# Performer attention, mixture of experts and squared-ReLU layer in one kernel: ten narrowing steps move to the end of a unit and to GpSimd's queue, and one token load is issued earlier

## The chip, the core and the metric

The kernel runs on one core of a Trainium2 chip. The core has five instruction streams that run side by side and meet at semaphores: TensorE (PE in the profile; PEld are its weight loads), VectorE (DVE), ScalarE (ACT), GpSimd (POOL) and SyncE (SP). Each stream executes its own instructions strictly in the order in which they were issued. Transfers are started by SP or by POOL and run on 16 shared DMA engines. The metric is device microseconds of one execution, from a median over runs; lower is better.

## The reference

Three parts follow one another, in float32: linear attention with an exponential feature map, a top-1 mixture of experts, and a feed-forward layer with a squared ReLU.

```python
def _attn_ref(q, k, v, omega):
    ...
    q_p, k_p = (phi(q_s), phi(k_s))
    kv = np.einsum('bhsm,bhsd->bhmd', k_p, v)
    ...
    return (num / den).astype(np.float32)

def _moe_ref(x, w_gate, w1, w2):
    ...
        h = np.maximum(xe @ w1[e], 0.0)
        ye = h @ w2[e]
        out[mask] = gate_w[mask, None] * ye

def _moe2_ref(x, w_in, w_out):
    h = np.maximum(x @ w_in, 0.0)
    return (h * h @ w_out).astype(np.float32)
```

There are 4 batches of 576 tokens, so 2304 tokens of width 512; the last layer has 2048 hidden units. The change concerns only the last layer, `h = relu(x @ w_in)` and `h * h @ w_out`, and there mostly its first product.

## The kernel before

**Stages.** Attention, then the experts (one expert per batch of tokens), then the last layer in two passes. Pass one computes the hidden values of the last layer and stores them to DRAM (`hscr`); pass two reads them back and multiplies by `w_out`. Every matmul operand is split into a rounded high part and a low rest (ACT copies the high part, DVE subtracts: `split`, L688), and each product is three matmuls: high x high, high x low, low x high.

**Pass one** is `first(u)` for units u = 0 to 15. A unit covers a pair of weight tiles for two batches and uses a seven-product scheme for 2x2 blocks. It has 14 *places*: place 2n+i is product n (0 to 6) for batch i (0, 1), six matmuls each, 84 in a unit. The products accumulate in PSUM banks X, Z and Y. Product 0 goes to X, and ACT copies X out as `p1` (`keep`, L920) before product 2 may accumulate onto the same bank. At product 5 DVE adds `Y + p1` (L959), which is the last read of that copy; the copy of the next unit goes to the same bytes of the tile `xT`. At product 3 DVE adds `Z + u2` (L954) into the buffer `h[i]`, which must first have been stored by the unit before (`hscr<-xT`, L966, from SP). The ReLUs with squares are L923 on DVE and L962, L963 on ACT.

**Work beside the matmuls.** After every place `self.extras(SA + 14 * u + 2 * n + i)` runs what the table in `plan` has put there. It is of four kinds:

- *Narrowing.* `w_in` and `w_out` arrive as float64 bits. `narrow_load` (L693) loads one half tile (512 KB, tile `wd`), `narrow` (L703) converts it (one ACT `Abs`, L715, then four DVE operations, L716 to L719) and stores 256 KB to `wscr`. 22 of the 32 are done in the expert stage. The other ten (`self.late`, odd numbers 13 to 31, halves of `w_out` that only pass two reads) are done in units 3 to 12, one per unit, at place 9. They share one buffer (`s0`) and one result buffer (`s1`). Their transfers are issued from SP: in SP's stream the store of one, the load of the next, then the two `hscr` stores of the unit.
- *Tokens.* Batch b, half c (here written token block (b, c)): `x_load` (L884) loads it, `x_sums` (L895) makes four sums on POOL (L69 to L72), `x_split` (L899) makes the high and low parts in four pieces. For b = 3 the load is issued from POOL. Blocks use two raw buffers in turn, so (3, 1) takes the place of (2, 1), and the first half of that place is free when pieces 0 and 1 of (2, 1) have been split.
- *Weight pairs.* `pair_load` (L632, two transfers from POOL), `pair_sums` (four sums on POOL, L60 to L63) and `pair_split`, for pairs p = 2 to 7 in units 2, 3, 6, 7, 10, 11 and the units after them.
- *Loads for pass two*, from place 13 of unit 12 on (`blocks_load`, from POOL).

Units 0 and 1 use batches 0 and 1, unit 2 is the first to use batches 2 and 3. What a place says is only where an instruction stands in each engine's stream: an engine that is idle runs ahead of the matmuls as far as its semaphores let it.

Of the kernel before, what the change touches and what calls it, by code (L numbers as in the profile page):

```python
# [9 lines left out]
I32 = mybir.dt.int32  # L10
# [8 lines left out]
DM = H * D  # L19
# [17 lines left out]
SA = 1000  # L37
# [52 lines left out]
class Kern:  # L90
# [602 lines left out]
    def narrow_load(self, c):  # L693

        f, i = divmod(c, 2)
        if c in self.late:
            st = self.more.tile([P, 2 * DM], F32, tag="s0", name=f"wd{c}", bufs=1).bitcast(I32)
        else:
            st = self.stage(f"wd{c}").bitcast(I32)
        self.nc.sync.dma_start(out=st, in_=self.a["wf"][f, :, i * DM : (i + 1) * DM].bitcast(I32))  # L700
        self.raw["d", c] = st

    def narrow(self, c):  # L703

        nc = self.nc
        f, i = divmod(c, 2)
        st = self.raw.pop(("d", c)).rearrange("p (n w) -> p n w", w=2)
        low, high = st[:, :, 0], st[:, :, 1]
        if c in self.late:
            r = self.more.tile([P, 2 * DM], I32, tag="s1", name=f"narrow{c}", bufs=1)[:, :DM]  # L710
        else:
            r = self.work.tile([P, DM], I32, tag="osb", name=f"narrow{c}", bufs=2)
        rf = r.bitcast(F32)
        v = nc.vector
        nc.scalar.activation(rf, high.bitcast(F32), AF.Abs)  # L715
        v.tensor_scalar(rf, rf, F64_LEAST, F64_MOST, op0=ALU.max, op1=ALU.min)  # L716
        v.tensor_scalar(r, r, 5, 2, op0=ALU.logical_shift_left, op1=ALU.logical_shift_right)
        v.scalar_tensor_tensor(r, high, -(1 << 30), r, op0=ALU.bitwise_and, op1=ALU.bitwise_or)
        v.scalar_tensor_tensor(r, low, 29, r, op0=ALU.logical_shift_right, op1=ALU.bitwise_or)  # L719
        nc.sync.dma_start(out=self.wscr[f][:, i * DM : (i + 1) * DM], in_=rf)  # L720


    def steps(self):
# [94 lines left out]
    def plan(self):  # L818
        ev = self.events = {}

        def at(s, *e):
            ev.setdefault(int(s), []).append(e)

        for f in range(5, NFE):
            at(f - 5, self.expert_split, 0, f)
        n_at = [4 + 45 * i // 21 for i in range(22)] + [SA + 14 * (3 + i) + 9 for i in range(10)]
        w_at = [5, 6, 7] + [s for s in range(8, 80) if s % 8 in (0, 2, 5, 6)]
        order = [2 * f for f in range(NFF)] + [2 * f + 1 for f in range(NFF)]
        self.late = order[22:]
        for n, c in enumerate(order):  # L830
            at(n_at[n] - (13 if c in self.late else 2), self.narrow_load, c)
            at(n_at[n], self.narrow, c)
        for i in range(24):
            b, f = 1 + i // NFE, i % NFE
            at(w_at[i] - 2, self.expert_load, b, f)
            at(w_at[i], self.expert_split, b, f)

        for i in range(4):
            b, c, u = i // 2, i % 2, 48 + 2 * i
            at(u, self.x_load, b, c)  # L840
            at(u + 2, self.x_sums, b, c)
            for j in range(4):
                at(u + 3 + j // 2, self.x_split, b, c, j)
        at(57, self.pair_load, 1, 0)
        at(58, self.pair_sums, 1, 0)
        for i in range(4):
            at(60 + i // 2, self.pair_split, 1, 0, i)

        at(61, self.pair_load, 1, 1)
        at(62, self.pair_sums, 1, 1)  # L850
        for i in range(4):
            at(SA + 2 + i, self.pair_split, 1, 1, i)
        beside = ((1, 4, 9, 10, 11, 12), (5, 9, 14, 15, 16, 17), (12, 16, 20, 21, 22, 23), (17, 21, 25, 25, 26, 27))
        for i, (l, m, *f) in enumerate(beside):
            b, c = 2 + i // 2, i % 2
            at(SA + l, self.x_load, b, c)
            at(SA + m, self.x_sums, b, c)
            for j in range(4):
                at(SA + f[j], self.x_split, b, c, j)
        for p in range(2, NP):  # L860
            u = SA + 14 * (4 * (p // 2 - 1) + 3 + p % 2)
            at(u - 6, self.pair_load, 1, p)
            at(u - 2, self.pair_sums, 1, p)
            for i in range(4):
                at(u + 1 + 2 * i, self.pair_split, 1, p, i)
        for p, l in enumerate((181, 183, 185, 187, 197, 201, 213, 217)):
            at(SA + l, self.blocks_load, p)
        for p in range(7):
            at(SA + (196, 199, 202, 207, 212, 216, 221)[p], self.blocks_split, p)
        for k, l, f in ((0, 204, 210), (1, 209, 219)):  # L870
            at(SA + l, self.h_load, k)
            at(SA + f, self.h_split, k)
        for s in ev:
            ev[s].sort(key=lambda e: ("load" in e[0].__name__) * (1 if e[0] in (self.narrow_load, self.expert_load) else 3) or 2)
# [415 lines left out]
```

## Time and profile before

| | |
|---|---|
| median of 3 runs | 771.57 us |
| the runs | 771.57, 771.61, 767.67 us |
| the profiled execution | 767.86 us, of which the span of instructions is 766.3 us |
| busy in the span | PE 740.9 us (97%), DVE 566.7 (74%), ACT 418.8 (55%), POOL 212.4 (28%) |
| pass one | 375.99 to 570.3 us in the span |
| issue to landing, medians | `we` (512 KB, POOL) 4.8 us, `wd` (512 KB, SP) 4.7, `hscr` store (576 KB, SP) 4.6, `wscr` store (256 KB, SP) 2.3 |

The profile has one profiled execution, so durations below come from that one, and its own time, 767.86 us, is near the lowest of the three runs. TensorE is the engine that is nearly always busy; the other engines' idle time matters only where TensorE waits for them. "Granted clock" is the share of TensorE's full clock, 2.4 GHz, in a stretch; it has a lower level of 1.2 GHz.

### The profile page before, as it was taken

The numbers are of one execution on the slowest core, as the hardware profiler recorded it, in microseconds if no ns is written. First come the engines' busy times: TensorE is split into PE (matmuls) and PEld (weight loads), VectorE is DVE, ScalarE is ACT, GpSimd is POOL, SyncE is SP. The second block draws the span as 40 slices with busy tenths as digits, with TensorE's granted clock in tenths as the row PEclk, the third lists the DMA queues.
The fourth block names the chain that finished last, engine by engine and source line by source line (L and its number), as shares of the span: only waits on it lengthen the run. The fifth ranks groups of instructions, "written<-read, shape, count | busy, mean of one in ns | idle before, by whom it ended". The sixth has DMA issues, their size and how long they took to land. (4 is left out here: it accounts for less than half of the span.)

```text
span 766.3 us, 15766 instructions
## 1 busy us (share of the span) xinstructions
PE 740.9 (97%) x5832; PEld 731.0 (95%) x5832; DVE 566.7 (74%) x1204; ACT 418.8 (55%) x1012; POOL 212.4 (28%) x272
## 2 busy tenths in 40 slices
PE   8999999999999999999988999899999999999995
PEld 7999999999999999999988999899999999999995
DVE  7788877876776667767395857676785899898783
ACT  5777776963554345535465545455573455454451
POOL 4666566831100010046265512201241110000000
PEclk9999998999999999999999999999999999999999
DMA  8756554645866766553244654645677464444330
GB/s 298 242 164 201 183 191 126 183 121 157 277 201 192 248 219 223 174 175 111 69 154 152 214 197 151 221 149 205 216 243 258 164 221 138 138 139 136 120 104 31
DMA packets 77108, 136.14 MB, mean 178 GB/s; under 512 B 8513, under 2 KB 37329, under 8 KB 77025
## 3 DMA queue, kind: packets, MB, share of 16 engines
q1 hardware_dynamic: 67584, 102.35, 40.5%
q0 software_dynamic: 9440, 32.73, 13.7%
q8 instruction: 48, 0.79, 0.4%
q14 instruction: 36, 0.29, 0.1%
HBM read 93.54 MB, written 41.50 MB: 176 GB/s over the span
## 5 line engine op out<-in xcount | busy, mean ns | idle before, releaser
L763 ACT ACTIVATE hh<-h 128x288 fp32r<-128x288 f32 x64 | 26.4, 412 | 98.0 <-PE h L753 97.9
L920 ACT COPY xT<-X 128x288 f32<-128x288 f32 x96 | 37.9, 403 | 54.8 <-PE X L946 32.8
L764 DVE SCALAR_TENSOR_TENSOR hl<-h,hh 128x288 fp32r<-128x288 f32 x64 | 29.1, 455 | 41.8 <-ACT hh L763 41.3
L1014 ACT CAST hc<-xT 128x384 fp32r<-128x384 f32 (+1 forms) x76 | 38.8, 563 | 28.5 <-DVE xT L63 20.4
L272 ACT ACTIVATE kp<-pj_kp,bias_kp 128x128 f32<-128x128 f32 x144 | 39.3, 397 | 25.1 <-DVE bias_kp L260 16.8
L618 POOL DMA_DIRECT2D we<-we x32 | 17.7, 552 | 121.1 <-DVE wB L612 54.3
L954 DVE TENSOR_TENSOR xT<-Z,xT 128x288 f32<-128x288 f32 x32 | 14.5, 456 | 44.5 <-DMA hscr<-xT 35.1
L657 POOL DMA_DIRECT2D xT<-wscr x32 | 17.2, 540 | 101.7 <-DVE w L691 43.0
L944 PE MATMUL X<-wA,w 128*128 128x288 f32 x128 | 39.0, 305 | 5.9 <-ACT xT L920 5.3
L1060 PE MATMUL y<-wB,hc 128*128 128x256 f32 x152 | 43.2, 284 | 0.0
L1058 PE MATMUL y<-wB,hc 128*128 128x256 f32 x152 | 43.1, 284 | 0.0
L1059 PE MATMUL y<-wB,hc 128*128 128x256 f32 x152 | 43.0, 283 | 0.0
L1016 DVE TENSOR_TENSOR hc<-xT,hc 128x384 fp32r<-128x384 f32 (+1 forms) x76 | 42.2, 617 | 0.0
L944 PE MATMUL X<-wB,w 128*128 128x288 f32 x128 | 38.2, 298 | 3.5 <-ACT wB L690 2.7
L272 ACT ACTIVATE qp<-pj_qp,bias_qp 128x128 f32<-128x128 f32 x144 | 39.3, 394 | 3.2 <-DVE bias_qp L260 1.6
L285 PE MATMUL kv_ps<-vin,kp 128*128 128x65 f32 (+1 forms) x320 | 40.6, 281 | 0.0
L285 PEld LDWEIGHTS kv_ps<-vin,kp 128*128 128x128 f32 (+1 forms) x320 | 38.9, 197 | 1.1 <-issue 0.3
L923 DVE SCALAR_TENSOR_TENSOR xT<-xT 128x288 f32<-128x288 f32 (+1 forms) x64 | 39.2, 644 | 0.0
L752 PE MATMUL h<-xl,wB 128*128 128x288 f32 x128 | 38.1, 298 | 0.9 <-DVE xl L740 0.9
L752 PE MATMUL h<-xl,wA 128*128 128x288 f32 x128 | 37.9, 296 | 0.4 <-DVE xl L740 0.4
L945 PE MATMUL X<-wB,w 128*128 128x288 f32 x128 | 37.9, 296 | 0.4 <-DVE wB L691 0.4
L780 PE MATMUL y<-hl,wA 128*128 128x288 f32 x128 | 37.9, 296 | 0.3 <-DVE hl L764 0.3
(240 smaller groups left out, 3070.7 us busy)
## 6 DMA issues: line engine op xcount, KB each, us to landing
hscr<-xT SPq DMA_DIRECT2D x32, 576.0 KB, 4.6
we<-we POOLq DMA_DIRECT2D x32, 512.0 KB, 4.8
wd<-wf SPq DMA_DIRECT2D x32, 512.0 KB, 4.7
xT<-hscr SPq DMA_DIRECT2D x64, 256.0 KB, 4.4
xT<-wscr POOLq DMA_DIRECT2D x48, 256.0 KB, 4.3
wscr<-narrow SPq DMA_DIRECT2D x32, 256.0 KB, 2.3
vin<-vv SPq DMA_DIRECT2D x18, 260.0 KB, 3.9
kpc<-kk SPq DMA_DIRECT2D x18, 256.0 KB, 3.0
```

Source lines behind the costliest of these rows:

```text
L272: nc.scalar.activation(y[:, h, :], ps[h // 4][:, h % 4 * M : (h % 4 + 1) * M], AF.Exp, bias=bias[:, h : h + 1])
L285: nc.tensor.matmul(self.kv_ps[b, i][:, j * VW : (j + 1) * VW], self.kp[t][lo:hi, 4 * i + j, :], self.vin[t][lo:hi, 4 * i + j, :], start=(t ...
L752: nc.tensor.matmul(ps, w1, xl, start=False, stop=False)
L780: nc.tensor.matmul(out, w1, hl, start=False, stop=False)
L920: nc.scalar.copy(v, ps)
L923: nc.vector.scalar_tensor_tensor(v, v, 0.0, v, op0=ALU.max, op1=ALU.mult)
L944: nc.tensor.matmul(ps, w1, xh[:, r, c], start=(start and c == 0), stop=False, skip_group_check=True)
L1014: nc.scalar.copy(hc[q].at(0, a, b), raw[:, q, a + 1 : b + 1])
L1016: nc.vector.tensor_tensor(hc[q].at(1, a, b), raw[:, q, a + 1 : b + 1], hc[q].at(0, a, b).bitcast(F32), ALU.subtract)
L1058: nc.tensor.matmul(ps, h1, w1, start=first, stop=False, skip_group_check=True)
L1059: nc.tensor.matmul(ps, h1, w2, start=False, stop=False, skip_group_check=True)
L1060: nc.tensor.matmul(ps, h2, w1, start=False, stop=last, skip_group_check=True)
```

## The change

Three edits to the table and the queues; no arithmetic is added or removed.

```diff
@@ narrow_load
-        self.nc.sync.dma_start(out=st, in_=self.a["wf"][f, :, i * DM : (i + 1) * DM].bitcast(I32))
+        queue = self.nc.gpsimd if c in self.late else self.nc.sync
+        queue.dma_start(out=st, in_=self.a["wf"][f, :, i * DM : (i + 1) * DM].bitcast(I32))
@@ narrow
-        nc.sync.dma_start(out=self.wscr[f][:, i * DM : (i + 1) * DM], in_=rf)
+        queue = nc.gpsimd if c in self.late else nc.sync
+        queue.dma_start(out=self.wscr[f][:, i * DM : (i + 1) * DM], in_=rf)
@@ plan
-        n_at = [4 + 45 * i // 21 for i in range(22)] + [SA + 14 * (3 + i) + 9 for i in range(10)]
+        n_at = [4 + 45 * i // 21 for i in range(22)] + [SA + 14 * (3 + i) + 13 for i in range(10)]
...
-            at(n_at[n] - (13 if c in self.late else 2), self.narrow_load, c)
+            at(n_at[n] - (8 if c in self.late else 2), self.narrow_load, c)
...
-        beside = ((1, 4, 9, 10, 11, 12), (5, 9, 14, 15, 16, 17), (12, 16, 20, 21, 22, 23), (17, 21, 25, 25, 26, 27))
+        beside = ((1, 4, 9, 10, 11, 12), (5, 9, 14, 15, 15, 16), (12, 17, 20, 21, 22, 23), (16, 21, 25, 25, 26, 27))
```

A row of `beside` holds the places of the load, the sums and the four splits of one token block, counted from the start of pass one.

First, the late narrowing steps on DVE. This is DVE's stream in unit 10 before: `narrow27` is the tile being converted, `Z10` and `Y10` are the PSUM banks of unit 10, `Z11` of unit 11.

```order
L954 TENSOR_TENSOR xT_113<-Z10_1_6529,xT_113 128x288
L957 TENSOR_TENSOR xT_113<-xT_113 128x288 x2
L716 TENSOR_SCALAR narrow27_6606<-narrow27_6606 128x512
L717 TENSOR_SCALAR narrow27_6606<-narrow27_6606 128x512
L718 SCALAR_TENSOR_TENSOR narrow27_6606<-wd27_6496,narrow27_6606 128x512
L719 SCALAR_TENSOR_TENSOR narrow27_6606<-wd27_6496,narrow27_6606 128x512
L959 TENSOR_TENSOR xT_113<-Y10_0_6530,xT_113 128x288
L923 SCALAR_TENSOR_TENSOR xT_113<-xT_113 128x288
L959 TENSOR_TENSOR xT_113<-Y10_1_6531,xT_113 128x288
```

And this is the same stretch of the changed kernel, in which line numbers are one higher from L701 on and two higher from L721 on (L956, L959, L961 and L925 are the L954, L957, L959 and L923 of before, L717 to L720 the L716 to L719).

```order
L956 TENSOR_TENSOR xT_113<-Z10_1_6527,xT_113 128x288
L959 TENSOR_TENSOR xT_113<-xT_113 128x288 x2
L961 TENSOR_TENSOR xT_113<-Y10_0_6528,xT_113 128x288
L925 SCALAR_TENSOR_TENSOR xT_113<-xT_113 128x288
L961 TENSOR_TENSOR xT_113<-Y10_1_6529,xT_113 128x288
L925 SCALAR_TENSOR_TENSOR xT_113<-xT_113 128x288
L925 SCALAR_TENSOR_TENSOR xT_113<-xT_113 128x576 x2
L717 TENSOR_SCALAR narrow27_6646<-narrow27_6646 128x512
L718 TENSOR_SCALAR narrow27_6646<-narrow27_6646 128x512
L719 SCALAR_TENSOR_TENSOR narrow27_6646<-wd27_6572,narrow27_6646 128x512
L720 SCALAR_TENSOR_TENSOR narrow27_6646<-wd27_6572,narrow27_6646 128x512
```

The four operations stood ahead of the two `Y + p1` additions; they now stand behind them and behind the last ReLUs of the unit. ACT's `Abs` moves in the same way, from ahead of the last two ReLUs to behind them, directly ahead of the first `p1` copy of the next unit.

Second, POOL's stream around unit 6 before: L637 are the two loads of a weight pair, L60 to L63 its sums.

```order
L63 TENSOR_TENSOR xT_113<-xT_113 128x256
L637 DMA xT_113<-wscr8_95 128x512
L637 DMA xT_113<-wscr9_96 128x512
L60 TENSOR_TENSOR xT_113<-xT_113 128x256
L61 TENSOR_TENSOR xT_113<-xT_113 128x256
```

And the same stretch of the changed kernel (L701 is the load and L722 the store of a narrowing step).

```order
L63 TENSOR_TENSOR xT_113<-xT_113 128x256
L722 DMA wscr6_93<-narrow13_5731 128x512
L701 DMA wd15_5794<-wf 128x1024
L722 DMA wscr7_94<-narrow15_5866 128x512
L701 DMA wd17_5921<-wf 128x1024
L722 DMA wscr8_95<-narrow17_5989 128x512
L701 DMA wd19_6044<-wf 128x1024
L637 DMA xT_113<-wscr8_95 128x512
L637 DMA xT_113<-wscr9_96 128x512
L60 TENSOR_TENSOR xT_113<-xT_113 128x256
L61 TENSOR_TENSOR xT_113<-xT_113 128x256
```

Each store and load now stands between the weight pairs in POOL's stream; each store waits there for DVE, and the next pair's loads stand behind it. SP's stream keeps only the `hscr` stores in these units.

Third, POOL's stream around the token blocks (3, 0) and (3, 1) before: L889 is a load, L69 to L72 the sums.

```order
L889 DMA xT_113<-yscr_104 128x2x576
L69 TENSOR_TENSOR xT_113<-xT_113 128x288
L70 TENSOR_TENSOR xT_113<-xT_113 128x288
L71 TENSOR_TENSOR xT_113<-xT_113 128x288
L72 TENSOR_TENSOR xT_113<-xT_113 128x288
L889 DMA xT_113<-yscr_104 128x2x576
```

And in the changed kernel, where the load is L891:

```order
L891 DMA xT_113<-yscr_104 128x2x576 x2
L69 TENSOR_TENSOR xT_113<-xT_113 128x288
L70 TENSOR_TENSOR xT_113<-xT_113 128x288
L71 TENSOR_TENSOR xT_113<-xT_113 128x288
L72 TENSOR_TENSOR xT_113<-xT_113 128x288
```

The second load, block (3, 1), stood behind the four sums of block (3, 0) and now stands ahead of them.

## Rows read from the trace of the kernel before

**Rows 1.** Busy time of each engine in pass one: us, busy (instructions), clock, DMA.

```profile
375.99:570.30 194.31, 184.99 (x1345) 182.40 (x1346) 138.87 (x255) 106.23 (x259) 58.69 (x74) 0.98 0.56 190
```

**Rows 2.** The late `Abs` instructions: group (ns, first and last start), and two in time order.

```profile
L715 ACT ACTIVATE narrow<-wd x10: 673/674/677, 425.1 to 533.1; 128x512 f32<-128x512 f32 x10
...
510.73 0.68 ACT L715 ACTIVATE narrow<-wd 128x512 f32<-128x512 f32 x1
...
521.93 0.67 ACT L715 ACTIVATE narrow<-wd 128x512 f32<-128x512 f32 x1
```

**Rows 3.** TensorE's waits from 410 to 570 us: total, times, longest.

```profile
PE X L944 <- ACT xT L920: 5.0, 5, 2.6
```

**Rows 4.** TensorE in order of time: start, us, instruction [idle before <-releaser].

```profile
403.69 0.40 PE L944 MATMUL X<-wB,w 128*128 128x288 f32 x1 [2.71 <-ACT wB L690]
404.48 0.40 PE L945 MATMUL X<-wB,w 128*128 128x288 f32 x1 [0.40 <-DVE wB L691]
408.51 0.40 PE L944 MATMUL X<-wB,w 128*128 128x288 f32 x1 [0.58 <-ACT xT L920]
...
492.62 0.40 PE L944 MATMUL X<-wA,w 128*128 128x288 f32 x1 [2.61 <-ACT xT L920]
...
539.80 0.40 PE L944 MATMUL X<-wA,w 128*128 128x288 f32 x1 [0.60 <-ACT xT L920]
```

**Rows 5.** ACT's waits from 420 to 545 us, and one copy in time order.

```profile
ACT xT L920 <- DVE xT L959: 18.9, 15, 4.4
...
492.17 0.40 ACT L920 COPY xT<-X 128x288 f32<-128x288 f32 x1 [4.43 <-DVE xT L959]
```

**Rows 6.** DVE in order of time in unit 8.

```profile
487.60 0.96 DVE L716 TENSOR_SCALAR narrow<-narrow 128x512 f32<-128x512 f32 x1
488.60 0.84 DVE L717 TENSOR_SCALAR narrow<-narrow 128x512 int32<-128x512 int32 x1
489.48 1.11 DVE L718 SCALAR_TENSOR_TENSOR narrow<-wd,narrow 128x512 int32<-128x512 int32 x1
490.62 1.09 DVE L719 SCALAR_TENSOR_TENSOR narrow<-wd,narrow 128x512 int32<-128x512 int32 x1
491.64 0.44 DVE L959 TENSOR_TENSOR xT<-Y,xT 128x288 f32<-128x288 f32 x1
```

**Rows 7.** The late narrowing operations on DVE, 420 to 545 us: ns minimum, median, maximum.

```profile
L716 DVE TENSOR_SCALAR narrow<-narrow x10: 416/419/965, 426.3 to 536.5; 128x512 f32<-128x512 f32 x10
L717 DVE TENSOR_SCALAR narrow<-narrow x10: 427/428/850, 426.8 to 536.9; 128x512 int32<-128x512 int32 x10
L718 DVE SCALAR_TENSOR_TENSOR narrow<-wd,narrow x10: 691/693/1266, 427.2 to 537.5; 128x512 int32<-128x512 int32 x10
L719 DVE SCALAR_TENSOR_TENSOR narrow<-wd,narrow x10: 691/692/1110, 428.0 to 538.2; 128x512 int32<-128x512 int32 x10
```

**Rows 8.** POOL in order of time beside it: a pair's first and last sum.

```profile
487.36 0.92 POOL L60 TENSOR_TENSOR xT<-xT 128x256 f32<-128x256 f32 x1 [4.82 <-DMA xT<-wscr]
...
490.12 1.05 POOL L63 TENSOR_TENSOR xT<-xT 128x256 f32<-128x256 f32 x1
```

**Rows 9.** Two stretches of 4 us with the granted clock (columns as in rows 1).

```profile
494.00:498.00 4.00, 4.00 (x22) 4.00 (x22) 0.98 (x2) 0.61 (x2) 0.00 (x0) 0.62 0.97 371
406.00:410.00 4.00, 3.42 (x20) 3.07 (x19) 3.15 (x4) 3.34 (x9) 2.60 (x4) 0.72 0.48 160
```

**Rows 10.** POOL's issue of the loads of token blocks (3, 0) and (3, 1).

```profile
390.71 0.74 POOL L889 DMA_DIRECT2D xT<-yscr  x1
...
398.87 0.73 POOL L889 DMA_DIRECT2D xT<-yscr  x1
```

**Rows 11.** ACT and DVE at the splits of (2, 1), then of (3, 1).

```profile
402.96 0.67 ACT L690 CAST wB<-xT 128x576 fp32r<-128x576 f32 x1 [3.57 <-DMA xT<-yscr]
...
393.00 2.45 DVE L691 TENSOR_TENSOR wB<-xT,wB 128x576 fp32r<-128x576 f32 x4
...
403.66 2.03 DVE L691 TENSOR_TENSOR wB<-xT,wB 128x576 fp32r<-128x576 f32 x2 [0.88 <-ACT wB L690]
```

**Rows 12.** The 32 loads of 512 KB issued from POOL in the expert stage.

```profile
L618 POOL DMA_DIRECT2D we<-we x32: 528/531/732, 96.2 to 317.5; - x32
...
DMA to landing us min/median/max: 3.8/4.8/7.6
```

## Prediction

> **What bounds the kernel now.** I first read the busy times by stage, then TensorE's waits, then, behind each wait, the engine that ended it. TensorE sets the pace; the change touches only pass one, so the question is what TensorE loses there. Pass one lasts 194.31 us [rows 1]. What it would last without any loss is read from the `Abs` instructions, one per unit: two that follow each other undisturbed start 11.20 us apart [rows 2]. That is 84 matmuls of 0.133 us, and 16 x 11.20 = 179.2, so 15.1 us are lost. The ten `Abs` lie 533.1 - 425.1 = 108.0 us apart where nine undisturbed units take 100.8 [rows 2], so 7.2 of the 15.1 fall between units 3 and 12. A wait of 0.60 and its restart in unit 13 follow [rows 4]: 0.8 with the restart. Some 7 us remain for units 0 to 2.
>
> The part from unit 3 on is one pattern. TensorE waits five times, 5.0 us in all, for ACT's copy of X [rows 3], that is for `p1`, ahead of product 2. ACT waits in turn for DVE's `Y + p1` of the unit before, 18.9 us in 15 waits [rows 5]; the longest TensorE wait, 2.61 [rows 4], follows the longest of these, 4.43 [rows 5]. And DVE is late with `Y + p1` because the four narrowing operations stand right ahead of it: in unit 8 they run from 487.60 to 491.7 and L959 starts at 491.64 [rows 6]. Undisturbed the four take 0.42 + 0.43 + 0.69 + 0.69 = 2.23 us by their medians [rows 7]; there they took 4.0, beside the sums of a weight pair on POOL, 487.36 to 491.2 [rows 8]. What the waits do not explain of the 8.0 is restarts and the clock: behind the 2.61 the clock was granted at 0.62 for 4 us and 22 matmuls ran where 30 fit [rows 9], 1.1 us in that window alone.
>
> The part in unit 2 is another wait: 2.71 us for ACT's split of token block (3, 1), 0.40 for DVE's, 0.58 for a copy [rows 4], and again a low clock, 0.72 [rows 9]. The load was issued at 398.87, behind the sums of (3, 0) [rows 10], and ACT could start at 402.96 [rows 11], 4.1 us later.
>
> **The change, part by part.**
>
> *Narrowing at the unit's end.* Nothing is added: the same ten `Abs` and forty DVE operations. With the four gone from ahead of it, L959 starts at least 2.2 us earlier, 4.0 where POOL's sums ran beside them. The largest lateness to be covered is 2.61 us, in the unit where they took 4.0; the others average (5.0 - 2.61) / 4 = 0.6, under 2.2. So all five waits go, with their restarts and the low clock: 7.2 + 0.8 = 8.0 us.
>
> What is late next? `Abs` now stands ahead of the next unit's first `p1` copy on ACT: 0.67 us [rows 2]. The copy is wanted by product 2, whose first matmul comes four places into the unit, 4 x 0.8 = 3.2 us; the first X is complete at 0.8 and the copy takes 0.40 [rows 5], so some 2 us are free, or 1.2 when the two squares and the `Abs` start only after the unit has begun. The 0.67 is hidden. On DVE the four operations lie where DVE otherwise waits for the `hscr` store to land before L954; 2.2 to 4.0 us fit ahead of it, since L954 needs product 3, 5.6 us into the unit. If that cover were gone, L954 would be late, then L959, as before.
>
> *The Pool queue.* Each unit's chain is: `Abs` 0.67, DVE 2.23, POOL's issue of the store about 0.8 (0.53 [rows 12] and, as an estimate, half of that until the next), then the next load, issue to landing 4.8 [rows 12]: 8.5 us, against the 11.20 until the next `Abs`. So the load lands 2.7 us early. With the four operations at 4.0 it is 10.3, still in time; with the longest landing, 7.6 [rows 12], and 4.0 together 13.1, 1.9 late, of which ACT's free 1.2 covers most. Behind the load on POOL stand a pair's two loads and sums, in units 6, 7, 10 and 11; before, POOL ran units ahead with them. They would be issued some 6 us into the unit, land by its end, and the four sums (3.8 us [rows 8]) end some 4 us into the next, where ACT wants the last of them between 4.8 and 6.4. That is tight, and ACT then waits rather than TensorE. For these places I put in 0.5 us; the bounds are 0 and, if each of nine units gave 0.7 back, 6.
>
> SP loses 20 issues between its `hscr` stores, which helps the stores and nothing else: priced at nothing. The loads for pass two stand behind the last store on POOL, about 4 us into unit 13; they are wanted from unit 14's first place on, 7 us later, and take 4.8: nothing.
>
> *The earlier token load.* It can go out when the first two of the four splits of (2, 1) have left DVE, which run from 393.00 to 395.45 [rows 11], so about 394.5 instead of 398.87: 4.3 us earlier, and ACT could start near 399. If that were all, the 2.71 + 0.40 + 0.58 = 3.7 would go, less some restart: at most 3. But DVE was waiting only 0.88 us for ACT there [rows 11]; it came to this split straight from other work, and TensorE needs DVE's low part too. So at most 0.9 can be won at that place. And the sums of (3, 1) now run on POOL beside DVE's work of 399 to 403, where before POOL was waiting for the load; two-input operations beside POOL's sums took 1.1 instead of 0.69 [rows 6, 7], which on six or so of them costs 2 us. The two nearly cancel: bounds 1 lost and 3 won; I take 0.4 won, because the later splits, which waited for POOL's sums, do come earlier. Moving pieces of (2, 1) one place up changes the order on neither DVE nor POOL: nothing.
>
> **Sum.** 767.86 - 8.0 - 0.4 + 0.5 = 760.0 us, against the profiled execution. The median of the three runs is 3.7 higher; two runs lie there and one with the profile. I know no reason for it in the trace, so I stay with the profile and let the range reach up.
>
> **Rivals.**
>
> *The token load pays in full* (0.08): DVE is not held by POOL's sums. Then 3 is won in place of 0.4: 757.4.
>
> *Part is given back* (0.14): the pairs' sums, now behind the narrowing on POOL, come late and ACT stalls at the pair splits ahead of its copies; or the clock falls again after a new wait. Price 3 to 6 of the 8: 763 to 766. For it speaks the 4.0 us of the four operations beside POOL's sums [rows 6, 8], which will meet again in the four pair units. Against it: in these units TensorE has 2 us of cover.
>
> *The narrowing is not the cause* (0.09): the lateness goes round through the `hscr` store, L954 and L959, and would stay if the stores took the time. Then 767.5. Against it: after unit 12, when no narrowing is left, only the wait of 0.60 is left, early in unit 13 [rows 4], and that one follows unit 12's narrowing.
>
> *The load comes late in every unit* (0.07), the one on the other side. POOL's load cannot go before the store ahead of it, and that waits for DVE; ACT waits for the load at `Abs`, and TensorE for the copy behind it. It decides from landing 2.7 + 1.2 = 3.9 us later than reckoned, about 8.7 us from issue; every us beyond costs nine. At 10.5 us the nine units lose 16, twice what is won: 776. Against it: 32 loads of this size from POOL landed in 7.6 at most, and none took over 0.73 to issue, beside a busy DVE [rows 12]. The Trainium skill (SBUF — State Buffer, section "SBUF: two separate sides") says that a DMA from GpSimd's queue starves while VectorE runs operations that use both its ports, since GpSimd cannot write the descriptors; it gives 3100 ns in place of 620. By that figure, as an estimate, store and load would be 5 us late together, past the 3.9, and the nine units would lose some 10: about 770. Rows 12 show no issue of that length here.
>
> **How the numbers follow.** The forecast, 757.5 to 763, has 0.62; predicted 760.0. The range that holds eight in ten takes in the token load's case below and most of what is given back above: 756 to 766.5. A difference of 0.5%, 3.9 us, is about what a measurement of this kernel can tell from none. Against the median, faster means below 767.7: the forecast, the full token load and nearly all of what is given back, 0.80. The same: 0.13, the case that narrowing is not the cause and part of the late loads. Slower, above 775.4: 0.07.
>
> **What would show it.** In the changed profile: TensorE's waits for L922 (the X copy) gone from unit 3 on; ACT's waits for L961 near zero; `Abs` 11.2 us apart throughout, with no wait for `wd<-wf`; no stretch of low clock behind unit 8; the load of (3, 1) issued near 394.5 and the wait in unit 2 about as long as before but put down to DVE. It is wrong if ACT waits for `wd<-wf` by more than 1.2 us in several units, if POOL's pair sums become what ACT waits for, or if the waits for L961 remain.

## The result, and the profile after

The changed kernel takes 762.37 us (median of 8 runs, 761.05 to 765.52), the kernel before 771.82 (8 runs, 767.67 to 774.77): a ratio of 0.9899, 95% interval 0.9877 to 0.9921, faster by 1.0%. Forecast were 760.0 us and a range of 756 to 766.5. The time came out as forecast; what follows shows that the main reason given for it left out what cost most.

The profiled execution took 761.62 us, with a span of 760.1. Line numbers are one higher than before from L701 on and two higher from L721 on (L956 is `Z + u2`, L961 `Y + p1`, L922 the copies, L946 to L948 the matmuls of pass one, L968 the `hscr` store). Pass one, with the columns of [rows 1]:

```profile
375.00:562.70 187.70, 182.71 (x1345) 181.81 (x1345) 140.30 (x254) 106.03 (x258) 67.47 (x94) 0.98 0.58 197
```

It lasts 187.7 us where it lasted 194.31 [rows 1]. The late `Abs` instructions, to compare with [rows 2]:

```profile
L716 ACT ACTIVATE narrow<-wd x10: 648/648/665, 429.3 to 530.1; 128x512 f32<-128x512 f32 x10
```

530.1 - 429.3 = 100.8 = 9 x 11.20: no unit from 3 to 12 loses anything. The list of waits from 410 to 570 us holds no line of PE where before there was the one of [rows 3]. Its lines on the stores and on POOL's store of the narrowing (what waited, for what: total, times, longest):

```profile
POOL wscr L722 <- DVE narrow L720: 68.0, 10, 12.7
...
DVE xT L956 <- DMA hscr<-xT: 1.9, 2, 1.3
```

The 68.0 us of POOL cost nothing, as POOL had nothing else to do. The 1.9 us stand in the line that matters. In the kernel before, the same list says this:

```profile
DVE xT L954 <- DMA hscr<-xT: 33.9, 19, 4.9
```

DVE waited 19 times for a store of the unit before to land, ahead of `Z + u2`. The prediction knew of this wait, since it put the moved operations into it, but did not ask what it cost: it went from TensorE to ACT to DVE and stopped at what DVE did, not at what DVE had waited for.

The line of POOL's ten late loads, from 410 to 545 us (issue, ns minimum, median, maximum; then the landing):

```profile
L701 POOL DMA_DIRECT2D wd<-wf x10: 537/537/554, 411.0 to 523.8; - x10
...
DMA to landing us min/median/max: 4.1/4.4/5.6
```

And the line of the ten stores of the narrowing:

```profile
L722 POOL DMA_DIRECT2D wscr<-narrow x10: 545/557/565, 432.6 to 533.4; - x10
```

No issue is longer than in [rows 12], and nobody waits for these loads.

Units 1 and 2 took 1.5 us longer than in the first profile of the kernel before. TensorE, to compare with [rows 4]:

```profile
396.79 0.40 PE L946 MATMUL X<-wA,w 128*128 128x288 f32 x1 [0.72 <-ACT xT L922]
398.29 0.40 PE L946 MATMUL X<-wA,w 128*128 128x288 f32 x1 [0.45 <-ACT xT L922]
401.00 0.40 PE L946 MATMUL X<-wB,w 128*128 128x288 f32 x1 [0.44 <-ACT wB L690]
404.76 0.61 PE L947 MATMUL X<-wB,w 128*128 128x288 f32 x1 [3.37 <-DVE wB L691]
```

The wait of 2.71 for ACT has become one of 3.37 for DVE. POOL, ACT and DVE there (L891 is the load of (3, 1)):

```profile
394.16 0.73 POOL L891 DMA_DIRECT2D xT<-yscr  x1 [3.51 <-issue]
...
400.27 0.67 ACT L690 CAST wB<-xT 128x576 fp32r<-128x576 f32 x1 [1.30 <-DMA xT<-yscr]
...
403.36 2.01 DVE L691 TENSOR_TENSOR wB<-xT,wB 128x576 fp32r<-128x576 f32 x2
```

The load is issued at 394.16 and ACT starts at 400.27, 6.1 us later; before it was 4.1 [rows 10, 11], and no run shows why it is longer. Counted from the start of pass one, it is issued 3.7 us earlier than before and has landed 1.7 us earlier. DVE comes to the split 3 us behind ACT. Behind TensorE's wait for it the granted clock falls (columns as in [rows 9]):

```profile
406.00:410.00 4.00, 4.00 (x19) 4.00 (x18) 1.75 (x4) 0.88 (x4) 1.95 (x3) 0.50 0.95 337
```

0.50 is the lower level, 1.2 GHz.

From the first matmul of each unit to the first of the next, worked out from TensorE's rows in order of time, over what 11.20 us a unit would take, the length of pass two, and the landing of the `hscr` stores issued from 410 to 545 us, for the kernel before, the changed one and the experiments, which are described below:

```
                        median   units   units   pass   stores land
                        us       1+2     3-13    two    median/max us
before                  771.8    +6.9    +8.1    196.0  4.3 / 6.0
before, once more       773.75*  +8.5    +10.1   195.4  4.6 / 6.6
changed                 762.4    +8.4    0.0     197.4  3.3 / 4.6
e1_narrow_only          761.4    +7.1    0.0     199.6  3.5 / 5.0
e2_tokens_only          773.6**  +8.2    +13.8   200.9  4.7 / 7.1
e3_place_only           759.4    +7.2    0.0     196.7  3.5 / 6.4
e4_queue_only           794.9    +7.5    +25.3   200.3  5.8 / 9.2
e5_no_late_load         760.7    +7.1    +0.9    195.1  3.8 / 5.6
e6_behind_y_load_ahead  788.9    +7.3    +27.9   198.0  5.9 / 8.1
e7_splits_early         757.9    +7.8    0.0     195.9  3.2 / 6.8
e8_no_last_sums         761.71*  +6.2    0.0     198.7  3.2 / 4.5
e10_sums_on_dve         762.4    +10.7   0.0     197.4  3.6 / 6.2
e11_load_behind         773.9    +8.7    +14.7   196.1  4.3 / 5.5
e12_load_on_pool        781.5    +9.0    +20.2   196.5  4.7 / 8.7
* one execution   ** its profiled execution, 780.54, is the longest of its 12
in e4_queue_only unit 14 lost another 4.3
```

Medians of different rows come from different chips; the ratios below compare each with the kernel before on its own chip. The other columns are from one profiled execution each, and such figures scatter: the kernel before, profiled twice, has 6.9 and 8.5 us in units 1 and 2, and the part ahead of pass one, the same program in all rows, took 372.7 to 378.8 us. The profiled execution of the change is 6.2 us shorter than that of before: 1.0 ahead of pass one, where the two programs are the same, 8.1 in units 3 to 13, less 1.5 in units 1 and 2 and less 1.4 in pass two. The 1.5 is no more than the scatter of units 1 and 2 just named.

### The profile page after: what moved, and what is told of

Same layout as the page of the kernel before. It is cut to its first block, busy times and chain, and to the rows that moved or that the text cites. A ratio compares the mean times of both kernels' runs of the same rounds, so it can differ in the third digit from the quotient of the medians.

```text
span 760.1 us, 15737 instructions
## 1 busy us (share of the span) xinstructions
PE 738.2 (97%) x5832; PEld 729.8 (96%) x5832; DVE 568.7 (75%) x1204; ACT 419.1 (55%) x1012; POOL 222.1 (29%) x292
## 5 line engine op out<-in xcount | busy, mean ns | idle before, releaser
L922 ACT COPY xT<-X 128x288 f32<-128x288 f32 x96 | 37.1, 400 | 38.5 <-PE X L948 38.3
L947 PE MATMUL X<-wB,w 128*128 128x288 f32 x128 | 38.4, 300 | 3.4 <-DVE wB L691 3.4
L925 DVE SCALAR_TENSOR_TENSOR xT<-xT 128x288 f32<-128x288 f32 (+1 forms) x64 | 40.2, 661 | 0.0
L946 PE MATMUL X<-wA,w 128*128 128x288 f32 x128 | 38.2, 298 | 1.7 <-ACT xT L922 1.2
L946 PE MATMUL X<-wB,w 128*128 128x288 f32 x128 | 38.4, 300 | 0.4 <-ACT wB L690 0.4
L753 PE MATMUL h<-xh,wA 128*128 128x288 f32 x128 | 38.2, 298 | 0.0
L948 PE MATMUL X<-wB,w 128*128 128x288 f32 x128 | 38.1, 297 | 0.0
```

The source lines that it names most:

```text
L753: nc.tensor.matmul(ps, w1, xh, start=(c == 0), stop=False)
L925: nc.vector.scalar_tensor_tensor(v, v, 0.0, v, op0=ALU.max, op1=ALU.mult)
L946: nc.tensor.matmul(ps, w1, xh[:, r, c], start=(start and c == 0), stop=False, skip_group_check=True)
L947: nc.tensor.matmul(ps, w1, xl[:, r, c], start=False, stop=False, skip_group_check=True)
```

## The experiments

**The parts one by one.** The first four kernels take the change apart.

```diff
 e1_narrow_only: the changed kernel with the old rows of tokens
-beside = ((1, 4, 9, 10, 11, 12), (5, 9, 14, 15, 15, 16), (12, 17, 20, 21, 22, 23), (16, 21, 25, 25, 26, 27))
+beside = ((1, 4, 9, 10, 11, 12), (5, 9, 14, 15, 16, 17), (12, 16, 20, 21, 22, 23), (17, 21, 25, 25, 26, 27))
 e2_tokens_only: the kernel before with the new rows of tokens (the same two lines, reversed)
 e3_place_only: e1, and the late transfers on SP (the same line in narrow_load and in narrow)
-queue = self.nc.gpsimd if c in self.late else self.nc.sync
+queue = self.nc.sync
 e4_queue_only: e1, and the places as before
-... [SA + 14 * (3 + i) + 13 for i in range(10)]
+... [SA + 14 * (3 + i) + 9 for i in range(10)]
-at(n_at[n] - (8 if c in self.late else 2), self.narrow_load, c)
+at(n_at[n] - (13 if c in self.late else 2), self.narrow_load, c)
```

Expected of e1_narrow_only:

> Only the narrowing edits (place 13, Pool's queue), token loads as before. Theory (the gain is the narrowing's, 8 us, and the token load gives nothing or costs 1 to 1.5 us in units 1 and 2): all units from 3 on last 11.2 us as in the changed kernel, units 1 and 2 last 12.3 and 17.0 as before, so the time is that of the changed kernel or about 1 us less: 760.5 to 762.5. Rival (the earlier token load brings a part of the gain): 763 to 766, between the two kernels.

Measured: 761.43 us (6 runs), ratio 0.9865 (0.9828 to 0.9901). All of the gain is in these two edits.

Expected of e2_tokens_only:

> Only the new row of token places, narrowing as before. Theory: within 1.5 us of the kernel before (770 to 773.5), with the five waits of units 5 to 13 still there and the load of block (3, 1) some 4 us earlier but TensorE's wait in unit 2 not shorter, now put down to DVE. Rival: 768 or less, the wait in unit 2 shorter by 2 us or more.

Measured: 773.57 us (12 runs), ratio 1.0011 (0.9981 to 1.0041): nothing won. TensorE's long wait in unit 2 was put down to DVE, as expected, and lasted 3.59 us.

Expected of e3_place_only:

> Narrowing at place 13 with its load at place 5, but its transfers left on SP's queue; tokens as before. Theory (what counts is where the four DVE operations stand, not the queue): as with Pool's queue, units 3 to 15 at 11.2 us, 760.5 to 763. Rival (the queue is part of the gain, since on SP the narrowing store waits for DVE ahead of the next loads and stores): the hscr stores or the loads come later and TensorE waits again for the X copies; 765 to 770.

Measured: 759.38 us (6 runs), ratio 0.9826 (0.9792 to 0.9861). The place of the narrowing and of its load gives everything; the interval lies below that of the whole change. Against e1 the intervals overlap, so that POOL's queue costs something at the new place is not shown.

Expected of e4_queue_only:

> Narrowing left at place 9, only its loads and stores moved to Pool's queue; tokens as before. Theory: the four DVE operations still stand ahead of Y + p1, so the waits for the X copies stay: 769 to 773, no gain. Rival (stores of hscr were held up on SP by the narrowing store ahead of them, and that was the lateness): DVE's wait for the hscr store shrinks and the time falls to 763 to 767.

Measured: 794.86 us (6 runs), ratio 1.0284 (1.0246 to 1.0321). This was a miss, and the one that showed that the theory lacked something: the four operations stand where they stood, and 22 us are lost. Its rows (POOL's issue of the late load, SP's of the two `hscr` stores, DVE's next `Z + u2`):

```profile
457.87 0.53 POOL L701 DMA_DIRECT2D wd<-wf  x1
...
459.27 1.00 SPq L968 DMA_DIRECT2D hscr<-xT  x2
...
466.49 0.46 DVE L956 TENSOR_TENSOR xT<-Z,xT 128x288 f32<-128x288 f32 x1 [6.65 <-DMA hscr<-xT]
```

The store takes some 7 us to land, DVE waits 6.65 for it, and all that follows is late by as much. Now the same rows of the kernel before, which had been there to read:

```profile
453.56 0.33 SPq L720 DMA_DIRECT2D wscr<-narrow  x1
453.98 0.38 SPq L700 DMA_DIRECT2D wd<-wf  x1
455.73 1.04 SPq L966 DMA_DIRECT2D hscr<-xT  x2
...
459.71 0.46 DVE L954 TENSOR_TENSOR xT<-Z,xT 128x288 f32<-128x288 f32 x1 [3.38 <-DMA hscr<-xT]
...
466.89 1.04 SPq L966 DMA_DIRECT2D hscr<-xT  x2
```

And DVE's first narrowing operation and its `Y + p1` in that round:

```profile
462.36 0.42 DVE L716 TENSOR_SCALAR narrow<-narrow 128x512 f32<-128x512 f32 x1
464.62 0.45 DVE L959 TENSOR_TENSOR xT<-Y,xT 128x288 f32<-128x288 f32 x1
```

This is a loop: the store is issued at 455.73 and has landed when DVE goes on at 459.71, the two `Z + u2` and the additions behind them take 2.7 us, the four narrowing operations 2.3, `Y + p1` and the ReLUs 2.3, and the next store goes out at 466.89. That is 11.16 us round, and a unit is 11.20, so a delay is not made good. Other rounds are longer: 13.0 and 14.0 us from unit 6 to 7 and from 7 to 8, with the narrowing beside a pair's sums on POOL [rows 6, 8]; the nine rounds from unit 3 to unit 12 average 12.15. In e4 one round took 13.3 us (446.00 to 459.27). The load of 512 KB goes out 1.75 us ahead of the stores; by this theory it is what makes them late.

**The load, the place on DVE, and the loop.** With that loop as theory 2:

```diff
 e5_no_late_load: the kernel before, in narrow_load
+        if c in self.late[1:]:
+            self.raw["d", c] = self.raw["d", self.late[0]]
+            return
 ... and in narrow the tile is kept for the next step
-st = self.raw.pop(("d", c)).rearrange("p (n w) -> p n w", w=2)
+st = self.raw["d", c].rearrange("p (n w) -> p n w", w=2)
 e6_behind_y_load_ahead: the kernel before, place 11, the next load right behind the store in narrow
-... [SA + 14 * (3 + i) + 9 for i in range(10)]
+... [SA + 14 * (3 + i) + 11 for i in range(10)]
+        if c in self.late[:-1]:
+            self.narrow_load(self.late[self.late.index(c) + 1])
 ... and in plan
-            at(n_at[n] - (13 if c in self.late else 2), self.narrow_load, c)
+            if c not in self.late[1:]:
+                at(n_at[n] - 2, self.narrow_load, c)
```

Expected of e5_no_late_load:

> The kernel before, narrowing at place 9 and its stores on SP, but nine of the ten late loads of 512 KB are left out: the narrowing steps of units 4 to 12 convert the first late tile again, with the same Abs, the same four DVE operations and the same store. In the kernel before each of these loads is issued about 1.8 us ahead of a unit's two hscr stores, and the stores take 4.6 us to land (median); where the load lies elsewhere they take 3.7. Theory 1 (the step of the prediction: the four DVE operations ahead of Y+p1 are the cause, the transfers do nothing): nothing changes, 768 to 773 us, and the waits of TensorE for the X copy stay near 5 us. Theory 2 (a loop: store, landing, Z+u2, narrowing, ReLU, store, some 11.2 to 11.4 us long against a unit's 11.2; the load beside the stores lengthens it by 0.9): the loop falls to about 10.4, the waits go although the narrowing stands where it stood, and the time is 760 to 763.

Measured: 760.7 us (6 runs), ratio 0.9883 (0.9842 to 0.9923). The narrowing stands ahead of `Y + p1` as before, and nearly the whole gain is there. DVE near the start of unit 9 (L722 is the last narrowing operation, L962 `Y + p1`):

```profile
483.60 1.11 DVE L722 SCALAR_TENSOR_TENSOR narrow<-wd,narrow 128x512 int32<-128x512 int32 x1
484.63 0.45 DVE L962 TENSOR_TENSOR xT<-Y,xT 128x288 f32<-128x288 f32 x1
```

And TensorE's only wait from 410 to 570 us, for a copy of X:

```profile
PE X L947 <- ACT xT L923: 0.4, 1, 0.4
```

Even here, beside POOL's sums, where the operation takes 1.11 in place of 0.69, `Y + p1` comes in time but for 0.4 us. Of the 8.1 us that units 3 to 13 lost, 0.9 are left with the order on DVE as it was; 7.2 need the loads (one execution against one; the second profile of the kernel before lost 10.1). The loop shows why: the first store of each pair landed in 4.07 us on average in units 3 to 11 of the kernel before and in 3.19 here, and the nine rounds average 11.24 in place of 12.15. Four of these rounds still take 11.9 to 12.5 us, three of them with the narrowing beside POOL's sums, but the other five take 10.2 to 11.0, so the delay is made good.

What is not shown is the other half: no run moves the four operations alone and leaves the load 1.75 us ahead of the stores. They are 2.3 us of the same loop, so taking them out might have been enough too.

Expected of e6_behind_y_load_ahead:

> The kernel before with the narrowing two places later, at place 11: behind both Y+p1 additions on DVE, but with its store and the next load still directly ahead of the two hscr stores on SP. Theory 1 (the order on DVE alone is the cause): 760 to 762 us, ACT's waits for Y+p1 near zero. Theory 2 (the loop through the hscr stores): the narrowing and the load are both still in the loop, so the stores still land in 4.6 us or more and Z+u2 still waits for them, but Y+p1 comes 2.2 us earlier in it, so TensorE is touched only once the lateness has grown over several units: 760 to 766, between the two. If the loop alone set the time, 768 to 773.

Measured: 788.92 us (6 runs), ratio 1.0240 (1.0201 to 1.0279), outside everything expected. SP's issues:

```profile
460.15 0.38 SPq L700 DMA_DIRECT2D wd<-wf  x1
460.64 0.39 SPq L969 DMA_DIRECT2D hscr<-xT  x1
```

And the waits from 410 to 570 us (L923 are the copies, L957 `Z + u2`, L715 `Abs`):

```profile
DVE xT L957 <- DMA hscr<-xT: 54.7, 20, 5.6
...
ACT narrow L715 <- DMA wd<-wf: 21.1, 10, 2.8
...
PE X L947 <- ACT xT L923: 8.9, 8, 2.3
PE Z L947 <- DVE xT L957: 8.8, 13, 2.3
```

Load and stores now go out within 0.5 us and land late together: the stores in 5.9 us, and `Abs` waits for the load too, 21.1 us. The loop's rounds take 12.8 to 15.8 us. The four operations stand behind both `Y + p1`, and yet the kernel is 2.4% slower, so their place ahead of `Y + p1` is not what costs most here. But this run does not test that place alone: the four still stand ahead of the store, and the load has moved from 1.75 to 0.5 us ahead of it.

**The load on the other side, and on the other queue.**

```diff
 e11_load_behind: the kernel before
-at(n_at[n] - (13 if c in self.late else 2), self.narrow_load, c)
+at(n_at[n] - (8 if c in self.late else 2), self.narrow_load, c)
 e12_load_on_pool: the kernel before, in narrow_load
-self.nc.sync.dma_start(out=st, ...)
+queue = self.nc.gpsimd if c in self.late else self.nc.sync
+queue.dma_start(out=st, ...)
```

Expected of e11_load_behind:

> The kernel before with one number changed, 13 to 8 places: the narrowing stays at place 9, ahead of Y+p1, and everything on SP, but the next late load stands behind the unit's two hscr stores on SP, about 0.5 us after them, in place of 1.8 us ahead. Theory (the load ahead of the stores lengthens the loop; the place of the narrowing on DVE doesn't matter): the stores land in 3.8 us or less, TensorE's waits for the X copy from unit 3 on are 1 us or less together, 760 to 764 us. Rival 1 (the order on DVE costs something by itself): 764 to 768. Rival 2 (a load close to the stores slows them on either side, or Abs now waits for the load, which lands 5 us after the stores' issue): 768 or more.

Measured: 773.93 us (11 runs), ratio 1.0065 (1.0042 to 1.0088). Rival 2 it is. The stores' median is still 4.3, though the first of a pair lands in 2.9 to 3.0 in six of the units 3 to 11; and a second loop has taken the place of the first, with ACT's wait from 410 to 570 us:

```profile
ACT narrow L715 <- DMA wd<-wf: 15.7, 8, 4.1
```

The load cannot go out before the stores, `Abs` waits for it, the narrowing for `Abs`, and the next stores for the narrowing. So with the narrowing at place 9 the load has no good side: it must lie within the loop, ahead of the stores or behind them. At place 13 it goes out in the middle of a unit. SP of e3_place_only:

```profile
449.00 1.17 SPq L968 DMA_DIRECT2D hscr<-xT  x2
452.73 0.33 SPq L722 DMA_DIRECT2D wscr<-narrow  x1
453.15 0.38 SPq L701 DMA_DIRECT2D wd<-wf  x1
460.20 1.17 SPq L968 DMA_DIRECT2D hscr<-xT  x2
```

The load goes out 4.2 us behind one pair of stores and 7.0 ahead of the next, longer than it takes to land; and the narrowing runs while the stores land, no longer between their landing and the next store.

Expected of e12_load_on_pool:

> The kernel before with the ten late loads, and they alone, issued from POOL; stores on SP and all places as before. It takes e4_queue_only (794.9 us) apart. There the load went out 1.4 us ahead of the hscr stores in place of 1.8, and from another queue than they. If the other queue is the cause (behind it on one queue the stores wait their turn, beside it on two they share the engines): the stores land in 5.5 us or more and the time is 785 to 796. If the shorter distance is the cause: the load, no longer behind the narrowing's store in its queue, goes out no later than before, the stores land in 4.3 to 4.8 us, and the time is 768 to 774.

Measured: 781.47 us (6 runs), ratio 1.0151 (1.0117 to 1.0186), between the two. Its rows:

```profile
455.19 0.53 POOL L701 DMA_DIRECT2D wd<-wf  x1 [11.40 <-DVE xT L960]
...
456.84 1.03 SPq L967 DMA_DIRECT2D hscr<-xT  x2
...
463.63 0.46 DVE L955 TENSOR_TENSOR xT<-Z,xT 128x288 f32<-128x288 f32 x1 [6.19 <-DMA hscr<-xT]
```

The load goes out 1.65 us ahead of the stores, about as before. The stores' median, 4.7 us, is near that of the kernel before in its two profiles, 4.3 and 4.6, but it mixes units: in the late ones the load stands 4.3 us ahead. In the four units with 1.65 to 1.68 us the first store landed in 4.8, 6.7, 3.8 and 6.6 us, where in the six units of the kernel before with 1.74 or 1.75 it landed in 3.4 to 5.3. So issuing the loads from POOL does harm by itself, about half of what e4 lost; the other half came with the narrowing's stores on POOL as well, which puts the load 0.25 us closer. The Trainium skill (DMA: Bandwidth & Descriptors, section "Queues, rings and completion order") says that a DMA engine takes packets in turn from the queues that it has work for, and works through the descriptors of one queue in their order. By that, a load on another queue takes turns with the stores; the later landings agree, but no run here looks at single packets.

**Units 1 and 2.**

```diff
 e7_splits_early: e3_place_only, and
+beside = (..., (5, 9, 14, 15, 15, 16), (12, 17, 19, 20, 22, 23), (16, 21, 23, 25, 26, 27))
 e8_no_last_sums: the changed kernel
     def x_sums(self, b, c):
+        if (b, c) == (3, 1):
+            return
 ... and in x_split
-        self.split(hi, lo, raw[:, k + 1 : e + 1])
+        at = (2 - (e - k) if i else 1) if (b, c) == (3, 1) else k + 1
+        self.split(hi, lo, raw[:, at : at + e - k])
 e10_sums_on_dve: e3_place_only, and
+beside = (..., (5, 9, 14, 15, 15, 16), (12, None, 19, 23, 23, 23), (16, None, 23, 24, 26, 27))
+for s, c, n in ((19, 0, (0, 1, 2, 3)), (23, 1, (0,)), (25, 1, (1, 2)), (26, 1, (3,))):
+    at(SA + s, self.x_sum, 3, c, n)        # x_sum: the sums of rights on DVE
```

Expected of e7_splits_early:

> The kernel of e3_place_only (759.4 us) with the load of (3,1) ahead of the sums as in the changed kernel, and besides one split of (3,0) ahead of the two Z+u2 and the first split of (3,1) ahead of the two Y+p1 of unit 1, so that DVE works in the 1.3 us in which it waits for the hscr stores, and TensorE's first need of (3,1) is not behind the ReLUs. Theory (in units 1 and 2 the order on DVE holds TensorE, since DVE had no gap from 396 to 408 us in the changed kernel): unit 2 takes 15 to 16.5 us in place of 17.2, and the time is 757 to 759. Rival (the load's landing holds it, 6.1 us in the changed kernel against 4.3): unit 2 stays at 17 to 18 and the time at 759.5 to 761.

Measured: 757.94 us (6 runs), ratio 0.9841 (0.9805 to 0.9878), not to be told from e3_place_only. Unit 2 took 17.3 us, as the rival said, though not for the rival's reason: the load had landed 2.2 us earlier than in e3_place_only, 25.0 us after the start of pass one, and TensorE waited for DVE instead. DVE and POOL there, then TensorE:

```profile
392.79 2.79 DVE L691 TENSOR_TENSOR wB<-xT,wB 128x576 fp32r<-128x576 f32 x1 [0.40 <-ACT wB L690]
...
392.65 0.81 POOL L69 TENSOR_TENSOR xT<-xT 128x288 f32<-128x288 f32 x1
...
399.15 2.31 DVE L691 TENSOR_TENSOR wB<-xT,wB 128x288 fp32r<-128x288 f32 x2
...
401.51 0.61 PE L947 MATMUL X<-wB,w 128*128 128x288 f32 x1 [2.67 <-DVE wB L691]
```

One subtraction of a split took DVE 2.79 us, where others of its size took 0.75, while three sums of POOL ran past it at 0.8 each. The two ahead of TensorE's wait, beside the sums of (3, 1), took 2.31 together, where 0.45 and 0.75 are usual.

Expected of e8_no_last_sums:

> The changed kernel without POOL's four sums of token block (3,1): its last three splits read loaded quarters in place of the sums, so the hidden values of these tokens are not the reference's. The prediction said that POOL's sums beside DVE eat what the earlier load gives. If so: DVE's operations from 399 to 404 us take 0.44 and 0.67 to 0.75 us as when alone, TensorE's wait for DVE's low part of (3,1), 3.4 us, falls to 1.5 or less, and unit 2 takes 15 to 16 us in place of 17.9. Rival (DVE is late because Z+u2 of unit 1 waits for the hscr stores of unit 0, beside which the early load runs): the wait and the unit stay within 0.7 us of what they are.

Measured, one execution: unit 2 took 15.6 us in place of 17.9, and TensorE's wait fell from 3.37 to 2.55:

```profile
404.35 0.40 PE L950 MATMUL X<-wB,w 128*128 128x288 f32 x1 [2.55 <-DVE wB L691]
```

Unit 2 took 17.0 us or more in each of the other 13 profiles, so the sums do cost time there, here 2.3 us, about the 2 that the prediction had put on them. But the wait did not fall to 1.5 as expected: most of it remains, with DVE still late at this split without the sums. Only 0.8 of the 2.3 lies in the wait; behind it the granted clock was 0.50 for 4 us in the changed kernel and 0.60 here. The execution as a whole was no shorter, 761.71: it lost 1.0 ahead of pass one and 1.3 in pass two.

Expected of e10_sums_on_dve:

> The kernel of e3_place_only, and besides for the token blocks (3,0) and (3,1): the four sums on DVE, one or two ahead of the split that needs them, in place of POOL; the load of (3,1) as early as in the changed kernel; the first split of (3,0) and its sums ahead of Z+u2, where DVE waits for the hscr stores; its other splits on ACT behind the u3 copies. Theory (units 1 and 2 lose their 7 us to the order on ACT and DVE and to POOL's sums beside DVE): unit 1 takes 11.2 to 11.8 in place of 12.4, unit 2 14 to 15.5 in place of 17.2, and the time is 755 to 757. Rival (the loads' landing sets unit 2, whoever makes the sums): unit 2 stays at 16.5 to 17.5 and the time at 758 to 760.

Measured: 762.42 us (6 runs), ratio 0.9901 (0.9869 to 0.9933), worse than e3. Unit 1 did fall to 11.35 us, and unit 2 rose to 21.8. The rows (L909 a sum on DVE, L932 the copies):

```profile
406.02 0.67 ACT L690 CAST wB<-xT 128x576 fp32r<-128x576 f32 x1 [2.65 <-DVE xT L909]
...
408.67 0.61 PE L956 MATMUL X<-wB,w 128*128 128x288 f32 x1 [4.27 <-ACT xT L932]
```

ACT stood at a split waiting for a sum on DVE, and the X copies of unit 2, which TensorE needed sooner, stood behind it. Neither the theory nor the rival had foreseen that.

**The kernel before, once more.** Expected of e9_before_again:

> The kernel before, unchanged, once more. Its median over many runs, 770 to 772 us, lies some 4 above the execution whose profile I have (767.9). Theory (the loop through the hscr stores is as long as a unit, so its lateness differs from one execution to the next): where this execution takes 770 or more, the difference lies in units 3 to 13, as further waits of TensorE for the X copy, and the hscr stores land later there. Rival: the difference lies ahead of pass one or in pass two.

Measured: 773.75 us. Its waits from 410 to 570 us:

```profile
DVE xT L954 <- DMA hscr<-xT: 31.9, 15, 3.9
...
PE X L944 <- ACT xT L920: 7.0, 3, 3.2
```

Its span is 5.8 us longer than that of the first profile: 2.9 ahead of pass one, 3.5 in pass one, 0.6 less in pass two. Units 3 to 13 lost 10.1 us in place of 8.1, at other places (mostly in 5 and 9, not 8 and 9), and units 1 and 2 lost 1.6 more. So the loop falls behind in one execution here and in another there, but that is only 2.0 of the 5.8 us. Theory and rival each have a part, and the 2.9 ahead of pass one and the 1.6 in units 1 and 2 stay unexplained.

## Why the prediction came out right, and where it was wrong

**The sum.** Narrowing: 8.0 expected, 8.1 found. Token load: 0.4 won expected, 1.5 lost. New places: 0.5 lost expected, nothing in pass one. Pass two: nothing expected, 1.4 lost. Ahead of pass one 1.0 was won where the program is unchanged, which is luck. Together that is 6.2 of the 7.9 forecast: 761.6 in the profile after. That units 3 to 13 lost just 8.1 to begin with is chance as well: in the second profile of the kernel before it was 10.1.

**The step that failed** is one that carried no number: "SP loses 20 issues between its `hscr` stores, which helps the stores and nothing else: priced at nothing." Without the late loads between the stores, 7.2 of the 8.1 are gone (e5). The size of the narrowing's term was right because it was read as the whole loss of units 3 to 13, and the change removes that loss whatever its cause. The reason given, that the four operations stand ahead of `Y + p1`, is left with 0.9 once the loads are out (e5), and moving them behind it with the load closer to the stores made things worse (e6). The four operations and the landing are parts of one loop, so 7.2 and 0.9 are not shares of two separate causes; what the order alone would give, with the load left where it was, has not been run. The signs that the prediction named for the narrowing came true, but they could not tell the two reasons apart: all of them lie behind the point at which DVE is late.

**The rival "the narrowing is not the cause"** named the loop, and I gave it 0.09 and 767.5 us. The mechanism was nearer the truth than mine; its price was wrong, because I did not see that the change takes both the load and the narrowing out of that loop. The argument against it, that only 0.60 is left once the narrowing ends [rows 4], can't tell the two apart, as the loads end a unit earlier.

**POOL's queue.** The chain was right: the load in unit 6 was issued at 455.54 and landed 4.8 later, 2.5 us ahead of the next `Abs`, at 462.89, where 2.7 was reckoned. Neither the late loads nor the pair sums behind them cost TensorE anything. The starved queue of the Trainium skill (SBUF — State Buffer, section "SBUF: two separate sides") was not met: 20 issues took 0.54 to 0.57 us beside a busy DVE, though no row shows which ports DVE's operations use there.

**The token load** went as argued, issued at 394.16 for the 394.5 reckoned, its wait put down to DVE, eaten by POOL's sums (2.3 us, e8). What was missed is that the load itself took 6.1 us in place of 4.1, and that DVE stays late without the sums. The 1.5 lost lie just beyond the bound of 1, but the kernel before differs by 1.6 there between its own two profiles, so that anything was lost is not shown.

**Pass two** is longer by 1.4, with a wait that the kernel before has not:

```profile
609.71 0.38 PE L1060 MATMUL y<-wA,hc 128*128 128x256 f32 x1 [0.78 <-ACT o L1075]
```

In the profiles with the late stores on POOL pass two took 197.4, 198.7, 199.6 and 200.3 us, in the others 195.1 to 198.1 and, in e2_tokens_only, 200.9. The same wait, between 0.6 and 3.2 us, stands in all of the first and in some of the others, e3_place_only with 0.9 among them. So the queue is not shown to be the cause, and the 1.4 us stay open.

## What to carry to other kernels

When an engine is late because of what it does, look one step further at what it waited for before it: a buffer that is stored, freed and filled again closes a loop, and its whole length, with the landing of the store in it, has to be compared with the period of the work. A transfer that nobody waits for is not free when it goes out just ahead of one on which such a loop depends; put it where it has landed before the next of those starts. And look for a sign that only the supposed cause would give: here the signs named for the narrowing would have come out the same with the other reason. In this kernel two numbers, place 13 and 8 places ahead, with all transfers left on SP (e3_place_only, 0.9826), were the better change than the whole one (0.9899).

## What the runs showed of the hardware

A store of 576 KB landed in 3.2 to 3.8 us by its median where no late load of 512 KB went out close to it, in 4.3 and 4.6 (two executions) with one some 1.75 us ahead on the same queue, and in 5.9 with one some 0.5 us ahead there (e6). With the load on another queue it was 4.7 where that went out 1.65 to 4.3 us ahead (e12), and 5.8 with 1.3 to 4.3 us (e4), where the narrowing's stores were on that queue too. A subtraction on DVE with two inputs took 2.79 us beside POOL's sums and 0.75 alone, while those sums took 0.8. The Trainium skill (SBUF — State Buffer, section "SBUF: two separate sides") says that the pair of ports is held by one engine for a whole instruction. The uneven split agrees with it.
